# Batch 0's phi by halves, its score copies on two engines, its second FFN1 in P's banks, and a last store in halves

## The chip, the core and the metric

The kernel runs on one core of a Trainium2 chip. The metric is the device time of one execution in microseconds (us); of several executions the median counts. Of the core's engines four matter: TensorE (PE, matmuls and transpositions), VectorE (DVE) and ScalarE (ACT), which convert, copy and do the pointwise work, and SyncE (SP), whose queue issues nearly all transfers. Each engine works through its own queue in order and waits there for what the others have to deliver.

## The reference

For 8 batches of 576 rows and 8 heads, 32 weights phi per row are turned by a softmax over all of the sequence into 32 mean keys and values per head; the rows attend to these means, and the result, 4608 rows of 512, goes through an FFN of width 2048 with SiLU.

```
a = phi - np.max(phi, axis=2, keepdims=True)
a = np.exp(a)
a = a / (np.sum(a, axis=2, keepdims=True) + 1e-09)
k_m = np.einsum('bhsm,bhsd->bhmd', a, k)
v_m = np.einsum('bhsm,bhsd->bhmd', a, v)
scores = scale * np.matmul(q, k_m.transpose(0, 1, 3, 2))
...
attn = attn / (np.sum(attn, axis=-1, keepdims=True) + 1e-09)
x = np.matmul(attn, v_m)          # then rows of 512 = heads x 64
h = x @ w_in
g = h * (1.0 / (1.0 + np.exp(-h)))
return g @ w_out
```

## The kernel before, in words

**The FFN sets the frame.** The kernel goes through the 8 batches, and in each through 16 slices of 128 columns of the FFN's width, called fc. For a slice, *FFN1* (ffn1, L593) makes the 128 hidden units for all 576 rows: two halves of 288 columns, six matmuls each, since every operand is split into a high and a low part and three of the products are needed. ScalarE applies the SiLU (silu, L613 for 512 rows; L615 for the 64 rows left over, into *gleft*), VectorE splits the result into a high and a low part (split, L605 and L607), and *FFN2* (ffn2, L627) adds 4 tiles x 3 matmuls to the accumulators *acc*. FFN2 of a slice runs behind FFN1 of the next one (prev, finish). The rows left over of two batches are gathered and done at the end of every second batch (left_step); a finished accumulator is copied out by ScalarE and stored over SP's queue (store, L633 and L636).

**P instead of x @ w_in.** x is attention times mean values, and so the kernel multiplies the mean values with w_in first: *P* (p_mm, L563, 16 matmuls into the two banks *bg*) has 32 rows per head. ScalarE writes its high part (L577), VectorE its low part (L579), both into *pparts*. FFN1 then multiplies pparts with the attention *aparts*, also in two parts. In batch 0, P is made in pieces of 256 columns, each of which needs one tile of w_in.

**The weights** come as 64-bit words and are converted on the chip during batch 0. w_in has eight tiles i0 to i7, w_out o0 to o7, of 256 of the 2048 hidden units each. The steps of a tile are called by letters (w_conv): p (L166) and c (L168) on ScalarE, s (L170) and a (L172) on VectorE, and for w_out also h (L174, *wo_hi*) on ScalarE and l (L176, *wo_lo*) on VectorE. I0 and O0 are converted in halves 0 and 1. The words land in three buffers *raw*; load_next issues a tile's load on SP when its place in the program is reached, and a load into a buffer waits until the conversion that reads it is done.

**Batch 0's attention** stands at the head of the program. *phi_max*, *phi_allmax* make a maximum over the sequence for each of the two halves p of phi (two transpositions and a broadcast on TensorE, L252 and L258), *phi_sub* (L291) subtracts it, *phi_exp* (L299, L302) takes the exponential, *e_mm* makes the mean keys and values (72 matmuls, L311 and L319) and divides them (L335, *kvn*). *f_tr* and *f_vt* transpose these (*kvT*). *f_scores(u)* (L448) makes the scores of half u of the rows, *f_copy(u)* (L461 for 2x256 columns into *sT*, L462 for the small rest into *sleft*) copies them out of PSUM, *f_turn(u)* (L473, L475) transposes them. Then come maximum, shift, exponential, sum and division (*f_max* L496, *f_sub* L501, *f_exp* L507, *f_sum* L511 to L513, *f_norm* L517), the way back (*f_back* L524, L532) and the two parts of the attention (*f_high* L542, *f_low* L545). The first FFN1 needs both. Between these, *keep_warm* (L79) gives TensorE matmuls whose result is not used.

**What sets the order.** The head of the program is a list of calls written out by hand (from L719). in_order ties the instructions of VectorE and ScalarE there to the order of the list, and those of TensorE and SP as well. Behind it, from slice 2 of batch 0, a table of slots (ev, events) says behind which half slice a piece of the next batch's attention, of P or a conversion (conv_next) stands; there a scheduler puts the instructions of VectorE and ScalarE in order, while TensorE and SP keep the program's order until the end of batch 0.

## Time and profile before

| | |
|---|---|
| median of 3 runs | 713.25 us (713.0 to 713.45) |
| the profiled execution | 711.86 us, its span 710.1 us |
| TensorE busy | 696.2 us, 98% of the span |
| VectorE busy | 366.3 us, 52% |
| ScalarE busy | 258.5 us, 36% |
| bytes moved | 60.14 MB, 85 GB/s on the mean |

The span runs from the first to the last instruction in the trace, and all times in it count from its start; the 1.76 us between span and execution lie around it. TensorE's busy share is an average over the whole span; the views below go by stretch. In a timeline a row stands for one instruction or a few of a kind in a row; "[1.70 <-ACT sleft L462]" says that the engine was idle for 1.70 us ahead of it, until ScalarE's L462 was done. Starts of neighbouring rows overlap a little, as instructions are pipelined.

### The profile page before, as it was taken

How to read it: one execution, taken by the hardware profiler on the slowest of the kernel's cores; microseconds unless marked ns; L12 is line 12 of the kernel's file. 1: busy time of each engine (PE TensorE's matmuls, PEld its weight loads, DVE VectorE, ACT ScalarE, POOL GpSimd, SP SyncE). 2: the span in 40 equal slices, each digit the busy share in tenths (PEclk: the TensorE clock that was granted, in tenths of full speed). 3: DMA queues.
4: the chain of work that ended last, by engine and by line, in shares of the span. 5: the costliest groups of instructions: out<-in, count | busy, mean ns of one | idle time of the engine just before them, and what ended most of it. 6: DMA issues, size and time to landing. Idle time of an engine off the chain costs nothing.

```text
span 710.1 us, 11571 instructions
## 1 busy us (share of the span) xinstructions
PE 696.2 (98%) x4833; PEld 556.1 (78%) x4833; DVE 366.3 (52%) x658; ACT 258.5 (36%) x454; POOL 0.7 (0%) x6
## 2 busy tenths in 40 slices
PE   7899999999999999999999999999999999999997
PEld 3577678788888788777887778887888878888885
DVE  3899886355353563538246373535635356233322
ACT  2789854233323332424224241423322323222211
POOL 0000000000000000000000000000000000000000
PEclk9999999999999999999999999999999999999999
DMA  9977615321113210232011420132101000010002
GB/s 341 387 243 235 245 38 224 135 67 35 45 31 135 67 34 1 83 146 68 1 60 20 153 76 3 61 135 67 34 15 60 2 1 1 0 61 1 1 1 74
DMA packets 25444, 60.14 MB, mean 85 GB/s; under 512 B 2096, under 2 KB 10416, under 8 KB 25392
## 3 DMA queue, kind: packets, MB, share of 16 engines
q1 hardware_dynamic: 24672, 57.02, 23.0%
q10 hardware_dynamic: 720, 2.38, 0.9%
q8 instruction: 38, 0.62, 0.4%
q14 instruction: 14, 0.11, 0.1%
HBM read 49.95 MB, written 9.44 MB: 84 GB/s over the span
## 4 chain that ended last, share of the span: by engine, by line
PE 83%; DVE 3%; ACT 2%; DMA 1%; issue 0%; ACTq 0%
PE acc L627 44%; PE h L593 25%; PE accleft L627 6%; PE bg L563 4%; PE bg L311 2%; PE bg L357 1%; DMA raw<-in_w_out 1%; DVE gparts L607 1%; ACT L613 1%; DVE phi L291 1%; ACT phi L299 0%; ACT pparts L577 0%; PE bg L319 0%; DVE qz L275 0%; ACT g L613 0%
## 5 line engine op out<-in xcount | busy, mean ns | idle before, releaser
L627 PE MATMUL acc<-wo_hi,gparts 128*128 128x512 f32 x1024 | 352.5, 397 | 0.3 <-DVE gparts L607 0.3
L627 PEld LDWEIGHTS acc<-wo_hi,gparts 128*128 128x128 f32 x1024 | 191.9, 188 | 66.9 <-issue 29.8
L593 PEld LDWEIGHTS h<-aparts,pparts 128*128 128x128 f32 x1536 | 215.2, 188 | 17.8 <-ACT gleft L615 4.7
L593 PE MATMUL h<-aparts,pparts 128*128 128x288 f32 x1536 | 225.9, 296 | 1.6 <-ACT gleft L615 0.8
L627 PE MATMUL acc<-wo_lo,gparts 128*128 128x512 f32 x512 | 201.2, 393 | 0.4 <-DVE wo_lo L176 0.4
L613 ACT ACTIVATE g<-h 128x512 f32<-128x512 f32 x128 | 76.4, 597 | 303.4 <-issue 175.4
L605 DVE CAST gparts<-g 128x512 fp32r<-128x512 f32 x128 | 54.5, 426 | 222.0 <-ACT g L613 221.2
L627 PEld LDWEIGHTS acc<-wo_lo,gparts 128*128 128x128 f32 x512 | 96.1, 188 | 15.2 <-DVE wo_lo L176 0.7
L607 DVE TENSOR_TENSOR gparts<-g,gparts 128x512 fp32r<-128x512 f32 x128 | 88.2, 689 | 10.5 <-DVE gparts L605 0.5
L579 DVE TENSOR_TENSOR pparts<-bg,pparts 128x1024 fp32r<-128x1024 f32 (+1 forms) x36 | 39.6, 1099 | 36.2 <-ACT pparts L577 36.2
L577 ACT ACTIVATE pparts<-bg 128x1024 fp32r<-128x1024 f32 (+1 forms) x36 | 33.4, 927 | 27.8 <-PE bg L563 27.8
L627 PE MATMUL accleft<-wo_hi,gparts 128*128 128x512 f32 x128 | 40.6, 389 | 0.0
L563 PE MATMUL bg<-win,kvT 64*32 64x512 f32 (+1 forms) x576 | 35.8, 554 | 0.9 <-DVE kvn L335 0.9
L615 ACT ACTIVATE gleft<-h 128x64 f32<-128x64 f32 x128 | 28.0, 218 | 0.0
L627 PEld LDWEIGHTS accleft<-wo_hi,gparts 128*128 128x128 f32 x128 | 24.0, 188 | 4.9
L633 ACT ACTIVATE o<-acc 128x512 f32<-128x512 f32 x32 | 19.2, 599 | 21.9 <-PE acc L627 10.7
L627 PE MATMUL accleft<-wo_lo,gparts 128*128 128x512 f32 x64 | 24.9, 389 | 0.0
L613 ACT ACT_TABLE_LOAD x14 | 18.0, 1283 | 8.0 <-PE h L593 7.9
L563 PEld LDWEIGHTS bg<-win,kvT 64*32 64x32 f32 x576 | 6.5, 104 | 14.1 <-issue 11.7
L605 DVE CAST gparts<-gleft 128x512 fp32r<-128x512 f32 x16 | 6.8, 427 | 20.3 <-PE accleft L627 11.9
L168 ACT ACTIVATE raw<-raw 128x1024 int32<-128x1024 uint32 (+1 forms) x16 | 16.7, 1041 | 0.0
L395 DVE TENSOR_REDUCE ssm<-sc 128x36 f32<-128x1152 f32 x7 | 9.5, 1354 | 8.8 <-ACT sc L391 8.8
(126 smaller groups left out, 365.6 us busy)
## 6 DMA issues: line engine op xcount, KB each, us to landing
kv<-in_kv SPq DMA_DIRECT2D x28, 516.0 KB, 5.7
q<-in_q SPq DMA_DIRECT2D x16, 576.0 KB, 3.8
out<-o SPq DMA_DIRECT2D x32, 256.0 KB, 2.1
raw<-in_w_in SPq DMA_DIRECT2D x14, 512.0 KB, 6.4
raw<-in_w_out SPq DMA_DIRECT2D x6, 1024.0 KB, 7.3
phi<-in_phi SPq DMA_DIRECT2D x7, 576.0 KB, 3.7
kv<-in_kv ACTq DMA_DIRECT2D x4, 516.0 KB, 6.0
kr<-in_kv SPq DMA_DIRECT2D x7, 258.0 KB, 7.2
```

The lines of the kernel that those rows point to most:

```text
L168: nc.scalar.activation(r, low, AF.Copy, scale=2.0**-29)
L311: nc.tensor.matmul(pt[p][M * r : M * (r + 1), :KVW], e[:, p, c, M * r : M * (r + 1)], kvt[c][:, p, r], start=c == 0, stop=False, skip_grou ...
L563: nc.tensor.matmul(bg[M * r : M * (r + 1), p, :w].rearrange("p (k f) -> p k f", f=P), kvT[D * p : D * (p + 1), 1, r], win[D * p : D * (p + ...
L577: nc.scalar.activation(hi[:, :, c], bg[:, :, :w], AF.Copy)
L579: nc.vector.tensor_tensor(lo[:, :, c], bg[:, :, :w], hi[:, :, c], op=ALU.subtract)
L593: nc.tensor.matmul(h[:, hf, :HALF], wt[:, p, fs], a[:, p, sl], start=n == 0, stop=n == 5)
L605: nc.vector.tensor_copy(ghi, g32)
L607: nc.vector.tensor_tensor(glo, g32, ghi, op=ALU.subtract)
L613: nc.scalar.activation(g32.rearrange("p (h f) -> p h f", h=2), h[:, :, :w], AF.Silu)
L615: nc.scalar.activation(gleft[:, fc, o : o + LEFT].rearrange("p (h f) -> p h f", h=2), h[:, :, w:HALF], AF.Silu)
L627: nc.tensor.matmul(acc[key], gt[:, cs], wt[:, fc], start=fc == 0 and n == 0, stop=fc == NFC - 1 and n == 2)
L633: nc.scalar.activation(o, acc.pop(key), AF.Copy)
```

## The change

In batch 0, phi's second half is no longer held back: each half is shifted and exponentiated right behind its own maximum (phi_sub works half by half, in all batches), and e_mm multiplies half 0 ahead of half 1. One of the two divisions goes to ScalarE. A half's scores are copied by ScalarE (256 columns and the rest) and VectorE (256 columns). The order of the list is another one: the warm-up matmuls are spread differently, both turns come ahead of f_vt, I0's second half is converted behind f_norm(0), O0's second half partly behind the first FFN1, I1 behind the second silu. The first FFN1 does the products with the attention's low part last (low_last), and the second FFN1 writes into the banks bg of P in place of h. On SP's queue the first load_next of three, w_in's tile 3, stands ahead of phi(1), the other two ahead of kv(1) and q(1, 0). The last store of the kernel is copied by ScalarE and VectorE, half each, and its two transfers go over the queues of SP and of ScalarE.

```
     def phi_sub(b, ps_=(0, 1)):
...
+        for p in ps_:
+            am = at[b]["am", p]
+            nc.vector.tensor_tensor(
+                e[:, p], e[:, p], am.unsqueeze(1).broadcast_to([P, FULLC, P]), op=ALU.subtract
+            )
+            nc.vector.tensor_tensor(er[rows(p)], er[rows(p)], am[rows(p)], op=ALU.subtract)
...
         turns = [(c, p) for c in range(FULLC) for p in range(2)]
+        if b == 0:
+            turns.sort(key=lambda t: t[1])
...
-            if b and p == 0:
+            if p == (b == 0):
                 nc.scalar.activation(kvn[:, :, p], src, AF.Copy, scale=rs[p])
...
-        nc.scalar.copy(t, first["st", u][:, :, : 2 * P])
+        nc.scalar.copy(t[:, 0], first["st", u][:, 0, : 2 * P])
+        nc.vector.tensor_copy(t[:, 1], first["st", u][:, 1, : 2 * P])
...
+    def ffn1(b, fc, h=None, low_last=False):
...
+        if h is None:
+            h = live["h"] = ps.tile([P, 2, 512], F32, tag="h", name="h", bufs=1)
+        kinds = ((hi, ahi), (hi, alo), (lo, ahi))
+        todo = [(hf, k) for hf in range(2) for k in range(3)]
+        if low_last:
+            todo = [(hf, k) for k in (0, 2, 1) for hf in range(2)]
...
+    def store(key, rows, last=False):
...
+        w = DMODEL // 2 if last else DMODEL
+        nc.scalar.activation(o[:, :w], a[:, :w], AF.Copy)
+        if last:
+            nc.vector.tensor_copy(o[:, w:], a[:, w:])
...
+            (nc.scalar if last and k else nc.sync).dma_start(out[r : r + n], o[at_ : at_ + n])
...
         for p in range(2):
             phi_max(0, (p,))
             phi_allmax(0, (p,))
-            keep_warm(idle, (5, 6)[p])
-        for p in range(2):
             phi_sub(0, (p,))
             phi_exp(0, (p,))
+            keep_warm(idle, (5, 2)[p])
         e_mm(0)
...
         f_copy(0)
-        w_conv(I0, 1, "pc")
+        keep_warm(idle, 2)
         f_turn(0)
         f_scores(1)
         f_copy(1)
-        f_vt()
-        f_turn(1)
+        spare = ps.tile([P, 512], F32, tag="acc", name="spare", bufs=NI)
+        keep_warm(spare, 2)
         f_max(0)
         f_sub(0)
-        w_conv(I0, 1, "sa")
+        f_turn(1)
+        f_vt()
         f_exp(0)
...
         f_sum(0)
+        f_norm(0)
+        w_conv(I0, 1, "pc")
+        f_back(0)
+        f_sum(1)
+        w_conv(I0, 1, "sa")
+        f_high(0)
+        w_conv(O0, 0, "pc")
+        keep_warm(spare, 7)
+        bg = p_mm(0, 0, CW, False)
         p_split(0, 0, CW, bg, (0,))
...
+        w_conv(O0, 0, "ha")
+        w_conv(O0, 1, "p")
+        h = ffn1(0, 0, low_last=True)
+        w_conv(O0, 0, "l")
+        gs = split(silu(0, 0, h))
+        w_conv(O0, 1, "c")
+        g32 = silu(0, 1, ffn1(0, 1, bgtile()))
+        w_conv(I1, None, "pcsa")
+        main_step(0, 0, gs, (0, 1))
+        g1 = split(g32, steps=(0,))
+        p_mm(0, CW, CW)
         w_conv(O0, 1, "sh")
...
+    load_next()
     load_phi(1)
+    load_next()
+    load_next()
     load_kv(1)
     load_q(1, 0)
-    for _ in range(3):
-        load_next()
```

What the new order does to the queues shows at three places.

**ScalarE from the first wo_hi to P's second piece.** The two rows of L613 (L626 now) are the silus of the first two slices; "L166 ... win<-raw 128x1024" and the L168 on raw 128x1024 are I1's two steps, and L577 (L582 now) writes P's high part. Before:

```order
L174 ACTIVATE wo_hi<-cva 128x512
L166 ACTIVATE win<-raw 128x1024
L613 ACTIVATE g_359<-h 128x512
L615 ACTIVATE gleft<-h 128x64
L168 ACTIVATE raw<-raw 128x1024
L174 ACTIVATE wo_hi<-cva 128x512
L613 ACTIVATE g_382<-h 128x512
L615 ACTIVATE gleft<-h 128x64
L577 ACTIVATE pparts<-bg 128x2x256
```

After:

```order
L174 ACTIVATE wo_hi<-cva 128x512
L166 ACTIVATE cva<-raw 128x512
L626 ACTIVATE g_355<-h 128x512
L628 ACTIVATE gleft<-h 128x64
L168 ACTIVATE raw<-raw 128x512
L626 ACTIVATE g_374<-bg 128x512
L628 ACTIVATE gleft<-bg 128x64
L166 ACTIVATE win<-raw 128x1024
L168 ACTIVATE raw<-raw 128x1024
L582 ACTIVATE pparts<-bg 128x2x256
L174 ACTIVATE wo_hi<-cva 128x512
```

I1's first step stood ahead of the first silu and its second step between the two silus; both now stand behind the second silu. O0's second wo_hi moved from ahead of the second silu to behind P's high part.

**VectorE from behind the first shift of the scores to the second division.** "fmx" and "fsc ... fmx" are f_max and f_sub, "fsm" and "fsc<-fsc,fsm" are f_sum and f_norm; "L170 win" and "L172 win" are the steps of I0's second half. Before:

```order
L170 TENSOR_SCALAR win<-win 128x512
L172 ISA win<-raw,win 128x1024
L496 TENSOR_REDUCE fmx<-firstu 128x20
L501 TENSOR_TENSOR fsc<-firstu,fmx 128x640
L511 TENSOR_REDUCE fsm<-fsc 128x16
L512 TENSOR_SCALAR fsm<-fsm 128x16
L513 RECIPROCAL fsm<-fsm 128x16
L517 TENSOR_TENSOR fsc<-fsc,fsm 128x512
L511 TENSOR_REDUCE fsm<-fsc 128x20
L512 TENSOR_SCALAR fsm<-fsm 128x20
L513 RECIPROCAL fsm<-fsm 128x20
L517 TENSOR_TENSOR fsc<-fsc,fsm 128x640
```

After:

```order
L501 TENSOR_REDUCE fmx<-firstu 128x20
L506 TENSOR_TENSOR fsc<-firstu,fmx 128x640
L516 TENSOR_REDUCE fsm<-fsc 128x16
L517 TENSOR_SCALAR fsm<-fsm 128x16
L518 RECIPROCAL fsm<-fsm 128x16
L522 TENSOR_TENSOR fsc<-fsc,fsm 128x512
L516 TENSOR_REDUCE fsm<-fsc 128x20
L517 TENSOR_SCALAR fsm<-fsm 128x20
L518 RECIPROCAL fsm<-fsm 128x20
L170 TENSOR_SCALAR win<-win 128x512
L172 ISA win<-raw,win 128x1024
L522 TENSOR_TENSOR fsc<-fsc,fsm 128x640
```

I0's two steps moved from ahead of f_max(1) to between f_sum(1) and f_norm(1).

**The score copies, with the semaphores that each waits for.** "Activation" is ScalarE's semaphore, "DVE" VectorE's, "PE" TensorE's, and "DMAHW" a transfer's; "sT" takes the scores' 2x256 columns and "sleft" the rest. ScalarE before:

```order
L461 COPY sT_233<-bg 128x512 [waits DMAHW3_49,PE_49]
L462 COPY sleft<-bg 128x2x32
L166 ACTIVATE win<-raw 128x512 [waits DMAHW3_49]
L168 ACTIVATE raw<-raw 128x512
L461 COPY sT_252<-firsts 128x512 [waits DMAHW4_49,PE_49]
L462 COPY sleft<-firsts 128x2x32
L441 COPY kvT_215<-firstt 128x128 [waits DVE_49]
```

ScalarE after:

```order
L465 COPY sT_228<-bg 128x256 [waits DMAHW3_49,PE_49]
L467 COPY sleft<-bg 128x2x32 [waits DVE_49]
L465 COPY sT_248<-firsts 128x256 [waits DMAHW4_49,PE_49]
L467 COPY sleft<-firsts 128x2x32 [waits DVE_49]
L445 COPY kvT_210<-firstt 128x128
```

VectorE after:

```order
L170 TENSOR_SCALAR win<-win 128x512 [waits Activation_49]
L172 ISA win<-raw,win 128x1024 [waits DMAHW6_49,DVE_49,Activation_49]
L466 COPY sT_228<-bg 128x256 [waits DMAHW3_49,Activation_49]
L466 COPY sT_248<-firsts 128x256 [waits DMAHW4_49,Activation_49]
L501 TENSOR_REDUCE fmx<-firstu 128x16
```

ScalarE's one copy per half has become a copy on ScalarE and one on VectorE; VectorE's waits for ScalarE, and ScalarE's copy of the rest waits for VectorE.

## Rows read from the trace of the kernel before

**Rows 1.** Page, parts 1 and 2: busy time by engine; clock by slice.

```profile
PE 696.2 (98%) x4833; PEld 556.1 (78%) x4833; DVE 366.3 (52%) x658; ACT 258.5 (36%) x454; POOL 0.7 (0%) x6
...
PEclk9999999999999999999999999999999999999999
```

**Rows 2.** Windows: length; busy time (instructions) PE, PEld, DVE, ACT, POOL; clock; DMA.

```profile
42.00:75.00 33.00, 31.83 (x270) 25.37 (x262) 29.95 (x49) 28.84 (x38) 0.00 (x0) 1.00 0.66 214
...
75.00:110.00 35.00, 34.55 (x259) 26.30 (x260) 30.34 (x43) 21.96 (x34) 0.00 (x0) 1.00 0.43 153
```

**Rows 3.** Timeline, TensorE, 0 to 20: start, length, instruction, idle before.

```profile
1.35 4.42 PE L79 MATMUL idle<-ident 128*128 128x512 bf16 x11 [1.35 <-POOL ident masks.py:199]
...
6.27 0.49 PE L258 MATMUL firstm<-ident,cm 128*128 128x128 f32 x2 [0.38 <-DVE cm L253]
...
11.04 1.75 PE L311 MATMUL first<-kv,phi 128*32 128x129 f32 x56 [0.36 <-ACT phi L302]
...
17.31 0.71 PE L448 MATMUL firsts<-q,kvT 64*32 64x288 f32 x16
...
19.73 0.66 PE L473 MATMUL firstu<-ident,sT 128*128 128x128 f32 x4 [1.70 <-ACT sleft L462]
```

**Rows 4.** Timeline, VectorE, 6 to 26.

```profile
6.13 0.42 DVE L240 TENSOR_TENSOR mt<-phi 128x256 f32<-128x256 f32 x1
...
13.72 0.61 DVE L335 TENSOR_SCALAR kvn<-first,rs 128x128 f32<-128x128 f32 x2
...
19.29 0.69 DVE L172 CUSTOM_DVE_ANT_0 win<-raw,win 128x1024 uint16<-128x1024 uint16 x1
...
25.32 0.83 DVE L517 TENSOR_TENSOR fsc<-fsc,fsm 128x640 f32<-128x640 f32 x1
```

**Rows 5.** Timeline, ScalarE, 17 to 24.

```profile
17.87 0.66 ACT L166 ACTIVATE win<-raw 128x512 f32<-128x512 f32 x1 [1.08 <-DMA raw<-in_w_in]
...
18.98 0.59 ACT L461 COPY sT<-firsts 128x512 f32<-128x512 f32 x1
...
19.55 0.29 ACT L441 COPY kvT<-firstt 128x128 f32<-128x128 f32 x1
...
23.00 1.28 ACT L755 ACT_TABLE_LOAD   x1
```

**Rows 6.** Timeline, TensorE, 27 to 44.

```profile
27.77 0.53 PE L593 MATMUL h<-aparts,pparts 128*128 128x288 f32 x2
...
30.91 1.85 PE L593 MATMUL h<-aparts,pparts 128*128 128x288 f32 x12 [0.80 <-ACT gleft L615]
...
32.60 0.39 PE L627 MATMUL acc<-wo_hi,gparts 128*128 128x512 f32 x1
...
34.08 0.66 PE L563 MATMUL bg<-win,kvT 64*32 64x256 f32 x16
...
42.01 1.85 PE L593 MATMUL h<-aparts,pparts 128*128 128x288 f32 x12
```

**Rows 7.** Timeline, ScalarE, 35 to 42.

```profile
35.85 1.14 ACT L166 ACTIVATE win<-win 128x1024 f32<-128x1024 f32 x1
...
40.00 0.62 ACT L613 ACTIVATE g<-h 128x512 f32<-128x512 f32 x1
...
41.43 0.25 ACT L615 ACTIVATE gleft<-h 128x64 f32<-128x64 f32 x1
```

**Rows 8.** Timeline, VectorE, 32 to 34.

```profile
32.66 1.23 DVE L172 CUSTOM_DVE_ANT_0 win<-raw,win 128x2048 uint16<-128x2048 uint16 x1
```

**Rows 9.** Timeline, ScalarE and then TensorE, 72 to 76.

```profile
72.18 1.14 ACT L166 ACTIVATE cva<-raw 128x1024 f32<-128x1024 f32 x1 [0.93 <-DMA raw<-in_w_out]
...
75.05 0.67 PE L563 MATMUL bg<-win,kvT 64*32 64x256 f32 x16 [0.85 <-DVE kvn L335]
```

**Rows 10.** Timeline, all engines and queues, from 705.

```profile
705.49 0.60 ACT L633 ACTIVATE o<-accleft 128x512 f32<-128x512 f32 x1 [9.61 <-PE accleft L627]
...
706.11 1.11 SPq L636 DMA_DIRECT2D out<-o  x2
```

More of the change, by code (lines that the diff above doesn't have):

```diff
@@ L586, in ffn1 @@
         ahi, alo = at[b]["ahi"], at[b]["alo"]
-        h = live["h"] = ps.tile([P, 2, 512], F32, tag="h", name="h", bufs=1)
-        for hf in range(2):
-            sl = slice(hf * HALF, (hf + 1) * HALF)
-            n = 0
-            for wt, a in ((hi, ahi), (hi, alo), (lo, ahi)):
-                for p in range(2):
-                    nc.tensor.matmul(h[:, hf, :HALF], wt[:, p, fs], a[:, p, sl], start=n == 0, stop=n == 5)
-                    n += 1
+        if h is None:
[4 more added lines that the diff above has]
+            todo = [(hf, k) for k in (0, 2, 1) for hf in range(2)]
+        n = [0, 0]
+        for hf, k in todo:
+            wt, a = kinds[k]
+            for p in range(2):
+                nc.tensor.matmul(
+                    h[:, hf, :HALF], wt[:, p, fs], a[:, p, hf * HALF : (hf + 1) * HALF],
+                    start=n[hf] == 0, stop=n[hf] == 5, skip_group_check=low_last,
+                )
+                n[hf] += 1
         return h
@@ L648, in left_step @@
         if n == NLS - 1:
[L649 removed]
+            store((b, "left"), [((b - 1) * S + MAIN, LEFT), (b * S + MAIN, LEFT)], b == B - 1)
     events = {}
@@ L724, in attn_ffn_kernel @@
             phi_allmax(0, (p,))
-            keep_warm(idle, (5, 6)[p])
-        for p in range(2):
             phi_sub(0, (p,))
             phi_exp(0, (p,))
+            keep_warm(idle, (5, 2)[p])
         e_mm(0)
         w_conv(I0, 0, "pc")
-        keep_warm(idle, 4)
+        keep_warm(idle, 3)
         f_tr()
```

47 lines of the change are left out of this document (10 added, 37 removed).

## The prediction

> **What bounds the kernel now.** I began with the page's busy shares: TensorE is busy for 98% of the span, at the full clock in every slice [rows 1]. The windows show where batch 0 and the start of batch 1 lose time: TensorE is idle for 1.17 us between 42 and 75 and for 0.45 between 75 and 110 [rows 2]; before 28 us much of what it runs are warm-up matmuls. So the time is a fixed stream of matmuls plus the moment at which that stream flows freely. An edit to batch 0 counts only by how much it shifts the FFN1 at 42.01 [rows 6], or a later one; a gain that a later wait swallows is worth nothing. I therefore read TensorE, VectorE and ScalarE in order of time through batch 0 and followed every step that the new order moves.
>
> **Phi by halves, and the means of k and v.** Half 0's broadcast is written at 6.27 + 0.49 = 6.76 [rows 3], so its shift can run there, and no longer only behind both halves' maxima. It now stands ahead of half 1's maxima (from 6.13 until now [rows 4]), which delays half 1's shift by between 0 and 0.9, the shift's own length with its remainder; I take 0.4, half of it, because TensorE was still busy with warm-up matmuls when half 1's maxima were done. Against that, half 0's 16 matmuls are done by then: 16 instead of 28 stand behind half 1's exponential, and 12 x 0.06 us (1.75 for 56 records, two a matmul [rows 3]) is 0.7. Net −0.3. The division, two in a row on VectorE (0.61 for both [rows 4]), now has one on each engine: −0.3. So the scores start 0.6 sooner.
>
> **The score copies.** ScalarE copied 512 columns in 0.59; 128 columns took 0.29 [rows 5], so 256 take about 0.39, and VectorE needs 0.42 for 256 columns [rows 4]. The changed program makes VectorE's copy wait for ScalarE's, and the small copy of the left part for VectorE's. So each pair costs 0.81 in a row, +0.2 each time; the copy by two engines doesn't do what it says.
>
> The Trainium skill (PSUM — Partial Sum Buffer, Specifications) says that ScalarE and VectorE can read PSUM in parallel as long as they keep to different banks. By it each pair would take 0.42 and f_max(1) would come 0.4 sooner; no row here shows the two side by side, and the program's own waits forbid it.
>
> What does help is that the conversion of I0's second half is gone from there: it waited 1.08 for its landing and held the second copy until 18.98 [rows 5], though the scores were written at 17.31 + 0.71 = 18.02 [rows 3]. Now the copies start at 18.02 − 0.6 + 0.2 + 0.1 = 17.7 and end at 18.55; before it was 19.57, so −1.0. On VectorE f_max(0) and f_sub(0) come only behind that second copy, for about 0.69 each (128x512 at that engine's pace for 640 columns, 0.83 [rows 4]), so f_max(1) starts near 19.85. Before, the turn that it reads ended at 19.73 + 0.66 = 20.4 [rows 3], its small part and the step to VectorE 0.1 later: −0.7 is left.
>
> **The moved conversion takes that back.** I0's second half now stands behind the table load, which ended at 23.00 + 1.28 [rows 5] and now ends 0.7 sooner, at 23.6. ScalarE's two conversions (0.66 each, the second starting 0.1 before the first ends) end at 24.85, VectorE's step (0.69 [rows 4]) at 25.6, and f_norm(1) waits behind it: 25.5 instead of 25.32. So the first FFN1, at 27.77 [rows 6], starts near 28.0: **the whole gain of 0.7 is gone, +0.2.**
>
> **Two FFN1s in a row.** The first no longer pauses for the low part of the attention, and the second has banks of its own, so it doesn't wait for the silu as it did (0.80 idle at 30.91 [rows 6]). With 1.69 a piece (30.91 to the first FFN2 at 32.60) the second ends at 28.0 + 3.4 = 31.4, against 32.6. −1.2 here; nothing has been given back yet.
>
> **The new wait.** P's next matmuls (34.08 [rows 6]) need w_in's tile I1. Before, its first conversion lay ahead of the first silu and its second right behind it, and VectorE's last step of it ran at 32.66 for 1.23 [rows 8]: ready at 33.9, when TensorE got there. Now all of I1 stands behind the second silu on ScalarE. From 31.5: silu 0.6 (0.62 [rows 7]; its left part ends beside the next step), two conversions at 1.04 (four of them fill 35.85 to 40.00 [rows 7]) and 0.1 for the last one's end, then VectorE 1.23 and 0.1 to TensorE: 31.5 + 0.6 + 2.1 + 0.1 + 1.23 + 0.1 = 35.6. P's matmuls are 1.5 later than before. TensorE has six FFN2 matmuls (1.48, 32.60 to 34.08) to fill 31.4 to 35.6 and stands idle for 2.7. Queued behind the wait are the other six FFN2s, and on the two other engines all that reads P.
>
> **What follows on ScalarE.** P is written at 35.6 + 0.66 + 0.1 = 36.35; its high part takes ScalarE 0.6 (128x512, as the silu [rows 7]), until 36.95, its low part VectorE 0.7 (a 128x512 of two inputs, as above), until 37.65, then the shift of O0's second half 0.4, and only then ScalarE's wo_hi 0.6, until 38.65. The four conversions of i2 and o1 follow (4.15): 42.7. From the silu that stands behind them to the end of the left part there were 1.68 us (40.00 to 41.43 + 0.25 [rows 7]), now until 44.35. The FFN1 that waits for that left part's banks starts at 44.4 instead of 42.01: **+2.4**. Before, the left part ended 0.3 ahead of that FFN1, so none of this is hidden. VectorE's wo_lo for O0, behind the same wait, also comes late, but ends sooner than this chain.
>
> **Loads.** On SP's queue i3, phi(1), o2 and i4 now stand ahead of kv(1) and q(1,0). i3 waits for the conversion of I0 (25.6), o2 for I1's (35.5), i4 for O0's; kv(1) and q(1,0) follow near 40 and are read only by batch 1's steps. i3 lands sooner but is converted behind o1 all the same; later tiles wait for buffers that come free with the late conversions. What this can give back is bounded: nothing at one end, at the other the 1.17 + 0.45 that TensorE idles between 42 and 110 [rows 2]. An example of it is 75.05, where it waited 0.85 because ScalarE had stood 0.93 for a landing at 72.18 [rows 9]. Modelled ends hide part of what is lost there, so for the range I allow twice the sum, 3.2. I take 0.5, near the lower end: the conversions keep their distance to the stream.
>
> **The tail.** The last copy takes 0.60 at 705.49, and two store issues on one queue 1.11 from 706.11 [rows 10]. The copy in halves is again one behind the other (0.39 + 0.42, +0.2), and both stores wait for the second half, but they issue together and save about 0.55: −0.35, between 0 and −0.55. Shifting later batches' phi in two pieces costs VectorE 0.1 a batch, beside a TensorE that is busy.
>
> **The sum.** 2.4 − 0.5 − 0.35 = +1.55. The profiled execution took 711.86 with a span of 710.1; it becomes 713.4. It is 1.4 below the median of the runs, 713.25, so the forecast for that is 714.8.
>
> **The rivals.**
> *The weights' stage gives more back.* ScalarE there stops waiting for landings, since i3 and o2 come without kv(1) and q(1,0) ahead of them. With all of the visible 1.6: 2.4 − 1.6 − 0.35, 713.7. For it speaks rows 9; against it that buffers come free late.
> *Faster.* The same place from a further point on: if every o tile has landed before ScalarE asks for it, nothing between 42 and 110 holds TensorE, and up to 3.2 comes back: 2.4 − 3.2 − 0.35 = −1.15, 712.1. It decides at the o tile that held ScalarE at 72.18: this landing must come a microsecond sooner against ScalarE's own order. Against it: its load is issued when an earlier tile's conversion ends, and that is later.
> *Worse.* These landings slip by as much as the stream, and ScalarE, now with the late conversions close behind each other, holds a silu: one more wait like 75.05's, +0.85, and no gain: 2.4 + 0.85 − 0.35, 716.1.
> *The clock.* Full clock is granted in every slice [rows 1], and TensorE's longest pause was 1.70, ahead of the second turn [rows 3]. The new pause is 2.7. If TensorE falls there from 2.4 to 1.2 GHz, and for as long as the first eleven warm-ups took, 4.42 (0.40 each [rows 3], though the record's clock is full there), half of that is lost: +2.2, 717.0.
>
> The Trainium skill (TensorE: Matmul & The Clock Gate, What's actually happening) says that the chip halves this clock after an idle stretch and gives it back after sustained work. By it the 2.7 may or may not be enough; nothing before shows a pause of that length.
>
> **How the numbers follow.** My forecast 0.44 (714.8, its own range 713.9 to 715.8), more given back 0.24 (713.7), faster 0.13 (712.1), worse 0.12 (716.1), the clock 0.07 (717.0). A measurement of this kernel tells about 0.2% from no change, that is 1.43 us: 711.8 and 714.7 are the borders. Faster holds most of its own rival, 0.10; slower the two last and a bit over half of the forecast, 0.47; 0.43 is left for no change. The range of 712.3 to 716.5 leaves out half of the fastest case and the clock's, with a little of the worse one.
>
> **What would show it.** VectorE's score copies start where ScalarE's end. f_norm(1) stands right behind an L172 near 25.5. TensorE idles for over 2 us until about 35.5, released by VectorE's L172 on win, and over 1 us ahead of the FFN1 near 44.4, released by gleft. From there the FFN1s of batch 0 are 1 to 3 us late, constant from about 95 on. The last two stores issue at the same time. I am wrong if the wait near 35.5 is under 1 us, or if the FFN1 after 95 stands where it stood.

## The result, and the profile after

The changed kernel took 715.4 us (median of 8 runs, 714.9 to 717.03), the kernel before 713.21 in the same runs (712.18 to 713.99). The ratio is 1.0034, with a 95% interval of 1.0023 to 1.0045: slower, by a little more than a measurement can tell from no change. The forecast was 714.8. The profiled execution of the changed kernel took 715.28, with a span of 713.5.

The page of the changed kernel, parts 1 and 2, answers to [rows 1]:

```profile
PE 696.6 (98%) x4829; PEld 557.6 (78%) x4829; DVE 368.2 (52%) x667; ACT 259.2 (36%) x455; POOL 0.7 (0%) x6
...
PEclk9989999999999999999999999999999999999999
```

TensorE is as busy as before, 696.6 us against 696.2. So the 3.4 us between the two spans are idle time and slow matmuls, and one digit of the clock line, the third, is below 9. The windows of the changed kernel (columns as in [rows 2], with one stretch more) show where:

```profile
33.00:42.00 9.00, 6.47 (x35) 5.12 (x36) 6.59 (x10) 5.30 (x7) 0.00 (x0) 0.62 0.39 127
42.00:75.00 33.00, 33.00 (x285) 26.75 (x284) 30.04 (x49) 29.35 (x39) 0.00 (x0) 1.00 0.80 280
75.00:110.00 35.00, 33.05 (x248) 24.68 (x247) 31.13 (x45) 24.14 (x35) 0.00 (x0) 1.00 0.42 149
```

From 33 to 42 us TensorE is idle for 2.53 us, and its mean granted clock is 0.62: for part of that stretch it ran at 1.2 GHz. From 42 to 75, where 1.17 us were idle before, none is; from 75 to 110 it is 1.95 in place of 0.45. TensorE's timeline tells the same (start, length, instruction, idle before and its releaser):

```profile
27.89 1.87 PE L603 MATMUL h<-aparts,pparts 128*128 128x288 f32 x12 [0.75 <-ACT aparts L547]
29.60 1.76 PE L603 MATMUL bg<-aparts,pparts 128*128 128x288 f32 x12
...
35.53 1.11 PE L568 MATMUL bg<-win,kvT 64*32 64x256 f32 x16 [2.70 <-DVE win L172]
...
39.29 2.79 PE L603 MATMUL h<-aparts,pparts 128*128 128x288 f32 x12
...
45.37 1.85 PE L603 MATMUL h<-aparts,pparts 128*128 128x288 f32 x12
...
82.14 0.44 PE L349 MATMUL h<-ident,kvn 128*128 128x128 f32 x2 [1.65 <-ACT gleft L628]
```

The first two FFN1s stand one behind the other, at 27.89 and 29.60, and end 1.4 us sooner than in [rows 6], where FFN2 began at 32.60 (now 31.19). Then P's second piece at 35.53 waits 2.70 us for VectorE's L172 on win, I1's last step; in [rows 6] it stood at 34.08, without a wait. It takes 1.11 in place of 0.66, and the FFN1 behind it, slice 2's, 2.79 in place of 1.93: these matmuls ran at the lower clock. The FFN1 of slice 3 starts at 45.37 in place of 42.01, with no wait ahead of it. And at 82.14 there is a wait of 1.65 us that the kernel before did not have.

ScalarE in the same kernel, around the pause and ahead of slice 3:

```profile
31.99 1.12 ACT L166 ACTIVATE win<-raw 128x1024 f32<-128x1024 f32 x1
32.99 1.13 ACT L168 ACTIVATE raw<-raw 128x1024 int32<-128x1024 uint32 x1
...
43.15 0.60 ACT L626 ACTIVATE g<-h 128x512 f32<-128x512 f32 x1
...
44.57 0.23 ACT L628 ACTIVATE gleft<-h 128x64 f32<-128x64 f32 x1
```

and VectorE's step that releases TensorE:

```profile
34.16 1.23 DVE L172 CUSTOM_DVE_ANT_0 win<-raw,win 128x2048 uint16<-128x2048 uint16 x1 [0.32 <-ACT raw L168]
```

I1's two steps on ScalarE run from 31.99, right behind the second silu, to 34.12; VectorE's last step begins at 34.16 and ends at 35.39. [rows 8] had it at 32.66. Slice 2's left part is done at 44.80, 0.57 ahead of slice 3's FFN1.

How far the stream of matmuls lies behind, slice by slice, is read from the starts of the FFN1s (timelines of TensorE; the kernel "before, tail" is an experiment below, whose batch 0 is that of the kernel before):

| FFN1 of batch 0's slice | before | before, tail | after | after against before |
|---|---|---|---|---|
| 0 | 27.77 | 28.43 | 27.89 | +0.12 |
| 2 | 36.17 | 36.84 | 39.29 | +3.12 |
| 3 | 42.01 | 42.66 | 45.37 | +3.36 |
| 9 | 75.64 | 76.72 | 77.24 | +1.60 |
| 10 | 81.98 | 83.08 | 84.86 | +2.88 |
| last of the kernel | 687.32 | 688.39 | 690.84 | +3.52 |

The profiled execution of the kernel before was an early one: VectorE's maximum of phi's second half began at 6.13 without waiting for its landing [rows 4], while in the two other profiles with this head (two experiments below) it began at 7.79 and 7.98, after waits of 1.01 and 1.68 for it. "Before, tail" is 0.66 later at slice 0 and 1.10 at slice 10. That is most of the 1.35 us by which this profile lay under the median, and why the profiles differ by 3.4 us and the medians by 2.2.

### The profile page after: what moved, and what is told of

The parts are those of the page before. It is cut to its first block, busy times and chain, and to the rows that moved or that the text cites. A ratio compares the mean times of both kernels' runs of the same rounds, so it can differ in the third digit from the quotient of the medians.

```text
span 713.5 us, 11577 instructions
## 1 busy us (share of the span) xinstructions
PE 696.6 (98%) x4829; PEld 557.6 (78%) x4829; DVE 368.2 (52%) x667; ACT 259.2 (36%) x455; POOL 0.7 (0%) x6
## 4 chain that ended last, share of the span: by engine, by line
PE 77%; DVE 8%; ACT 5%; issue 1%; DMA 1%; ACTq 0%; DVEq 0%
PE acc L640 42%; PE h L603 24%; PE accleft L640 5%; PE bg L568 3%; PE bg L315 2%; DVE gparts L620 1%; ACT L626 1%; PE bg L361 1%; DVE phi L294 1%; ACT phi L301 1%; ACT g L626 1%; DMA raw<-in_w_out 1%; ACT pparts L582 1%; DVE gparts L618 1%; DVE qz L276 1%
## 5 line engine op out<-in xcount | busy, mean ns | idle before, releaser
L626 ACT ACTIVATE g<-h 128x512 f32<-128x512 f32 x127 | 75.9, 598 | 305.5 <-issue 175.4
L582 ACT ACTIVATE pparts<-bg 128x1024 fp32r<-128x1024 f32 (+1 forms) x36 | 33.4, 927 | 30.9 <-PE bg L568 30.9
L168 ACT ACTIVATE raw<-raw 128x1024 int32<-128x1024 uint32 (+1 forms) x16 | 16.7, 1046 | 0.0
```

The lines of the kernel that those rows point to most:

```text
L168: nc.scalar.activation(r, low, AF.Copy, scale=2.0**-29)
L582: nc.scalar.activation(hi[:, :, c], bg[:, :, :w], AF.Copy)
L626: nc.scalar.activation(g32.rearrange("p (h f) -> p h f", h=2), h[:, :, :w], AF.Silu)
```

## The experiments

In all of them the ratio is to the kernel before, run on the same chip.

### I1 sooner again

```
         w_conv(O0, 1, "p")
+        w_conv(I1, None, "p")
         h = ffn1(0, 0, low_last=True)
...
         w_conv(O0, 1, "c")
+        w_conv(I1, None, "csa")
         g32 = silu(0, 1, ffn1(0, 1, bgtile()))
-        w_conv(I1, None, "pcsa")
```

> The changed kernel with one part undone: I1's first ScalarE step stands ahead of the first silu and its second between the two silus, as before the change. Theory (I1 behind the second silu sets the 2.70 us pause at 35.53, and the half-rate stretch from 34.77 to 41.60 follows from that pause): the pause shrinks to about 1 us, P's second piece starts near 33.7, the clock stays at 2.4 GHz, the FFN1 of slice 3 starts near 42.9 in place of 45.37, and the time falls by 2 to 2.9 us, to 712.5 to 713.4. Rival (the loads' new order sets the time further on, at the 1.65 us wait at 82.14): the gain at slice 3 is swallowed there, and the time falls by less than 0.8 us, to 714.6 or more.

It took 713.69 us; the ratio is 1.0013 (1.0004 to 1.0022), against the changed kernel's 1.0034 a gain of 1.5 us. That lies between the two forecasts. TensorE's timeline:

```profile
33.84 0.67 PE L568 MATMUL bg<-win,kvT 64*32 64x256 f32 x16 [0.83 <-DVE win L172]
...
42.66 1.85 PE L603 MATMUL h<-aparts,pparts 128*128 128x288 f32 x12 [0.97 <-ACT gleft L628]
...
79.65 0.45 PE L349 MATMUL h<-ident,kvn 128*128 128x128 f32 x2 [2.19 <-ACT gleft L628]
```

and a window behind the last of these rows:

```profile
75.00:84.00 9.00, 6.81 (x42) 4.39 (x41) 7.21 (x10) 6.49 (x10) 0.00 (x0) 0.81 0.88 320
```

The pause is 0.83 in place of 2.70, P's piece starts at 33.84, and slice 3 at 42.66, 2.7 sooner. Up to there the theory holds. But at 79.65 the wait for gleft has grown from 1.65 to 2.19, and behind it the clock fell (0.81 on the mean of 75 to 84). The rival was right that part of the gain is swallowed there, though not most of it: slice 10 is still 1.4 nearer to the first FFN1 than in the changed kernel (55.59 against 56.97). The fall of the clock is not in every execution: of the eleven, eight had a granted clock of 0.999 or 1.0 on the mean of the whole execution, and three, the profiled one among them, 0.996 or 0.997.

### Warm-up matmuls in the pause

```
+        gap = ps.tile([P, 512], F32, tag="acc", name="gap", bufs=NI)
+        keep_warm(gap, 11)
         p_mm(0, CW, CW)
```

> The changed kernel with 11 more warm-up matmuls (a result that nobody reads, into a free accumulator bank) ahead of P's second piece, so that TensorE is busy in the pause before 35.53 and nothing else moves. It separates the pause from the clock. Theory (the clock fell because of the pause, but ScalarE's chain bounds slice 3 anyway): P's second piece still starts near 35.5, the clock stays at 2.4 GHz, the FFN1 of slice 3 starts at 44.4 to 44.9 in place of 45.37 and waits there for gleft, and the time falls by 0.4 to 1.0 us. Rival (the clock is most of the loss): 6.07 us at half rate come back, 3 us, and the time is that of the kernel before. Second rival (the clock fell for another reason than the pause): the half-rate stretch stays and the time with it.

715.34 us, ratio 1.0039 (1.0027 to 1.0051): no gain. TensorE's timeline, and the window of the pause:

```profile
33.40 2.55 PE L79 MATMUL gap<-ident 128*128 128x512 bf16 x11
36.31 0.67 PE L568 MATMUL bg<-win,kvT 64*32 64x256 f32 x16 [0.36 <-DVE win L172]
...
45.13 1.05 PE L603 MATMUL h<-aparts,pparts 128*128 128x288 f32 x6 [0.98 <-ACT gleft L628]
```

```profile
33.00:42.00 9.00, 8.25 (x54) 5.27 (x53) 6.27 (x10) 5.75 (x7) 0.00 (x0) 1.00 0.37 122
```

The clock stays full, and P's piece takes 0.67 again. This execution's first FFN1 stands at 28.62, so distances from there compare: slice 3 comes 16.51 behind it, against 17.48 in the changed kernel (45.37 − 27.89). The fall of the clock thus cost 0.97 at slice 3, as expected, and now TensorE waits there, 0.98 for gleft. But at slice 10 only 0.3 is left (56.65 against 56.97, timelines), and in the time nothing that the two intervals could tell. So the pause was the clock's cause in this place, and most of the clock's price was hidden by waits further on: the first rival is out, and so is the second; the theory holds at slice 3 and fails at the end.

### The loads in their old order

```
-    load_next()
     load_phi(1)
-    load_next()
-    load_next()
     load_kv(1)
     load_q(1, 0)
+    for _ in range(3):
+        load_next()
```

> The changed kernel with the loads behind the list in the order of before: phi(1), kv(1), q(1,0), then three tiles of weights. Theory formed from the changed kernel's trace (the new order brings i3 and o2 sooner, which gives 1.76 us back between 45 and 77, but brings kv(1) later, which costs 1.29 at 82.14): FFN1s up to slice 9 are 0.4 to 1.0 later than in the changed kernel, the wait at 82.14 goes, and the time falls by 0.8 to 1.4 us, to 714.0 to 714.6. Rival (the prediction's: the order gives back about 0.5 and nothing is lost to it): the time rises by 0.5, to 715.9.

713.79 us, ratio 1.0014 (1.0004 to 1.0025): by the ratios 1.4 less than the changed kernel, as the theory formed after the result has it, and against the prediction. TensorE's timeline:

```profile
36.24 1.11 PE L568 MATMUL bg<-win,kvT 64*32 64x256 f32 x16 [2.71 <-DVE win L172]
...
81.21 0.44 PE L349 MATMUL h<-ident,kvn 128*128 128x128 f32 x2 [0.32 <-ACT gleft L628]
```

The pause is still 2.71, and P's piece again takes 1.11; but the wait that stood at 82.14 is 0.32. Slice 9 comes no later: 49.05 behind the first FFN1 (77.64 − 28.59), against 49.35 in the changed kernel. But the low clock lasted less long here (0.81 on the mean of 33 to 42, in place of 0.62), so the way from the FFN1 of slice 3 to that of slice 9 compares better: 32.14, against 31.87 in the changed kernel. The first experiment and the next but one ("Both undone") differ by the order of the loads alone, and their clock was full up to slice 9: 31.56 with the new order, 32.25 with the old. So the sooner i3 and o2 give back 0.3 to 0.7 there and not the 1.76 of the theory; the rest has another source (below). The other half holds. In the changed kernel the loads of kv(1) are issued at 41.4, between the weights' tiles, and not at 21.7. The transfer of w_out that was issued next to them (out<-in, engine, count, KB each, us to landing) took in the changed kernel

```profile
raw<-in_w_out SPq DMA_DIRECT2D x1, 1024.0 KB, 7.8
```

and with the old order

```profile
raw<-in_w_out SPq DMA_DIRECT2D x1, 1024.0 KB, 4.9
```

at nearly the same time of issue, 50.36 and 50.16. From 48 to 50 the DMA engines were busy all the time in the changed kernel (share 1.00) and idle with the old order (0.00). ScalarE in the changed kernel:

```profile
58.24 1.15 ACT L166 ACTIVATE cva<-raw 128x1024 f32<-128x1024 f32 x1 [0.78 <-DMA raw<-in_w_out]
...
80.38 1.12 ACT L168 ACTIVATE raw<-raw 128x1024 int32<-128x1024 uint32 x1
81.40 0.58 ACT L626 ACTIVATE g<-h 128x512 f32<-128x512 f32 x1
```

It waits for the late tile and begins that conversion at 58.24; with the old order that step ran at 55.16. Every tile behind it is then converted later, until the silu of slice 9 stands behind the two steps of another conversion: it starts 4.16 behind the start of its FFN1 (77.24), with the old order 2.80 (80.44 and 77.64), and TensorE stands at 82.14.

### I1 later in the kernel before

```
-        w_conv(I1, None, "p")
         gs = split(silu(0, 0, ffn1(0, 0)))
-        w_conv(I1, None, "csa")
         w_conv(O0, 1, "sh")
         g32 = silu(0, 1, ffn1(0, 1))
+        w_conv(I1, None, "pcsa")
```

> The kernel before with one part of the change alone: all of I1's conversion behind the second silu. Theory: P's second piece (34.08 before) waits for I1, TensorE stands for about 2.5 us near 36, the FFN1 of slice 3 starts 2.4 us later or more, near 44.4, and the time rises by 2 to 3.5 us, to 715.2 to 716.7, with a half-rate stretch behind the pause if the pause is as long as in the changed kernel. Rival (the pause is covered by slack that lies further on, in the loads): the time rises by under 0.7 us.

715.08 us, ratio 1.0033 (1.002 to 1.0046): this part alone makes the kernel before as slow as the whole change does. TensorE's timeline and the window:

```profile
37.73 0.67 PE L563 MATMUL bg<-win,kvT 64*32 64x256 f32 x16 [2.71 <-DVE win L172]
```

```profile
35.00:42.00 7.00, 4.28 (x37) 3.25 (x37) 5.09 (x8) 4.92 (x6) 0.00 (x0) 1.00 0.98 349
```

A pause of 2.71, released by the same L172. The clock stayed full in this execution, though the pause is as long as in the changed kernel. Slice 3 starts 16.51 behind the first FFN1 (45.13 − 28.62), 2.27 more than the 14.24 of the kernel before (42.01 − 27.77): the 2.4 of the forecast, from this part alone.

### Both undone

The edits of the first and the third experiment together.

> The changed kernel with two parts undone at once: I1's conversion as before the change (a1) and the order of the loads as before (a3). Theory (two separate losses, the pause at 35.53 and the wait at 82.14, and each hides behind the other when only one is undone): the FFN1 of slice 3 starts about 0.7 later than in the kernel before, the one of slice 10 about 1.2 sooner, no pause over 1.2 us is left behind 30, the clock stays at 2.4 GHz, and the time is 1.0 to 1.6 us below that of the kernel before, 711.4 to 712.2. Rival (the new order of batch 0 itself is late, whatever is undone): the time stays above the kernel before, 713.3 or more, as in a1 and a3 alone.

711.68 us, ratio 0.9988 (0.9979 to 0.9997): faster than the kernel before. TensorE's timeline:

```profile
34.31 0.67 PE L568 MATMUL bg<-win,kvT 64*32 64x256 f32 x16 [0.85 <-DVE win L172]
...
43.12 1.85 PE L603 MATMUL h<-aparts,pparts 128*128 128x288 f32 x12 [0.99 <-ACT gleft L628]
...
79.14 0.44 PE L349 MATMUL h<-ident,kvn 128*128 128x128 f32 x2 [0.52 <-ACT gleft L628]
```

Behind 30 no pause is over 1 us, and the clock stays full. From its first FFN1 (28.46) slice 3 comes 14.66 later, 0.42 more than in the kernel before, and slice 10 comes 53.09 later in place of 54.21. Against the changed kernel's ratio of 1.0034, one part undone took off 0.0021, the other 0.0020, and both together 0.0046. So two losses made the result, I1 behind the second silu and the loads, and they add up rather than hide each other; without them the rest of the change is a small gain.

### The score copies side by side

To the kernel above, with the last accumulator copied by ScalarE alone and its two stores on two queues:

```
+            t = [ps.tile([P, 512], F32, tag="acc", name=f"firsts{p}", bufs=NI) for p in range(2)]
...
+        nc.scalar.copy(t[:, 0], st[0][:, : 2 * P])
+        nc.vector.tensor_copy(t[:, 1], st[1][:, : 2 * P])
+        nc.scalar.copy(lv[:, 0, u], st[0][:, 2 * P : HALF])
+        nc.vector.tensor_copy(lv[:, 1, u], st[1][:, 2 * P : HALF])
```

> The kernel of the run above with two more edits. The scores of the second half are written into two tiles of one PSUM bank each in place of one tile of two, so that the program lets ScalarE's and VectorE's copies run side by side; and the last accumulator is copied by ScalarE alone, its two stores still on two queues. Theory (the copies were serialised only because both read one tile): VectorE's copy of the second half starts within 0.1 us of ScalarE's in place of 0.40 behind it, the first FFN1 starts 0.3 to 0.45 sooner, the end of the last matmul to the end of the span shrinks by 0.2 to 0.3, and the time is 0.5 to 0.75 below that run, 710.8 to 711.6. Rival (the two engines read PSUM one after the other anyway): the copies overlap in the program but take longer each, to about 0.8 for the pair, and the first FFN1 starts at the same time.

711.74 us, ratio 0.9983 (0.9973 to 0.9992). The two copies of the second half, ScalarE's and VectorE's:

```profile
18.21 0.37 ACT L471 COPY sT<-firsts 128x256 f32<-128x256 f32 x1 [1.12 <-PE firsts L456]
```

```profile
18.25 0.42 DVE L472 COPY sT<-firsts 128x256 f32<-128x256 f32 x1 [0.94 <-DMA raw<-in_w_out]
```

They run side by side and take 0.37 and 0.42, as long as one behind the other in the changed kernel (below). So the wait came from the one tile that both read, not from the chip. The Trainium skill (PSUM — Partial Sum Buffer, Specifications) says that ScalarE and VectorE can read PSUM in parallel as long as they keep to different banks; this trace agrees, with these two durations. The first FFN1 came 0.25 sooner than in the run above (28.21), with phi's second half at the same time (8.05 and 8.08), a little less than expected, and that was lost again: at slice 10 TensorE waits, which it did not above.

```profile
82.82 1.86 PE L610 MATMUL h<-aparts,pparts 128*128 128x288 f32 x12 [1.02 <-ACT kvT L351]
```

### I0's second half in its old place

```
         f_copy(0)
+        w_conv(I0, 1, "pc")
...
         f_sub(0)
+        w_conv(I0, 1, "sa")
...
-        w_conv(I0, 1, "pc")
         f_back(0)
         f_sum(1)
-        w_conv(I0, 1, "sa")
```

> The changed kernel with I0's second half converted where it was before the change: its ScalarE steps behind the first score copy, its VectorE steps behind the first shift. Theory of the prediction (the moved conversion takes back the gain of 0.7 ahead of f_norm(1)): without it f_norm(1) comes 0.5 to 0.9 sooner, the first FFN1 starts near 27.4 and the time falls by up to 0.5. Rival (the old place is worse in the new order, since the words of that half land near 17.6 only, and ScalarE's second score copy then waits behind them): the second copy ends 1 to 2 us later, the first FFN1 starts near 29.5 to 30, and the time rises by 1.5 to 2.5, to 717 or more.

717.56 us, ratio 1.0064 (1.0047 to 1.008): the rival was right. ScalarE's first step of that half, and TensorE around it:

```profile
18.46 0.66 ACT L166 ACTIVATE win<-raw 128x512 f32<-128x512 f32 x1 [1.90 <-DMA raw<-in_w_in]
```

```profile
20.68 0.65 PE L478 MATMUL firstu<-ident,sT 128*128 128x128 f32 x4 [2.58 <-ACT sleft L467]
...
21.28 4.66 PE L79 MATMUL spare<-ident 128*128 128x512 bf16 x13
```

The words land only at 18.46, ScalarE's copy of the second scores stands behind that step, and TensorE waits 2.58 for it. The clock fell there (0.66 on the mean of 21 to 26): thirteen warm-up matmuls take 4.66 us. In the changed kernel they took 2.97:

```profile
19.35 2.97 PE L79 MATMUL spare<-ident 128*128 128x512 bf16 x13
```

The first FFN1 starts at 30.48.

### The halved last store alone

The part of the change in store, in the kernel before.

> The kernel before with the halved last store alone. Theory: batch 0 stays as it is; behind the last matmul ScalarE's copy of 256 columns (0.39) and VectorE's (0.42) stand one behind the other, the two stores issue together 0.9 behind the start of the first copy, and from the start of the copy to the end of the span it is 0.1 to 0.35 shorter than in the kernel before (4.61 from 705.49 to 710.10). Rival: the two queues' stores land no sooner than one queue's, and that stretch is as long or longer by the 0.25 that the copies add.

One execution of 712.8 us, span 711.0. Its end:

```profile
706.57 0.39 ACT L635 ACTIVATE o<-accleft 128x256 f32<-128x256 f32 x1 [9.61 <-PE accleft L627]
706.99 0.42 DVE L637 COPY o<-accleft 128x256 f32<-128x256 f32 x1 [4.84 <-ACT o L635]
707.44 0.47 SPq L640 DMA_DIRECT2D out<-o  x1
```

VectorE's copy stands behind ScalarE's, as the program's waits say. From the first copy's start to the end of the span it takes 4.43 in place of 4.61 (705.49 to 710.10). The copies cost 0.25 more (0.87 to the issue in place of 0.62) and the stores end 0.43 sooner behind their issue (3.56 in place of 3.99).

### One FFN1 at a time

Two kernels: the one with I1 and the loads as before, and the changed kernel, each with the second FFN1 in h, behind the first silu, as in the kernel before:

```
-        h = ffn1(0, 0, low_last=True)
+        h = ffn1(0, 0)
...
-        g32 = silu(0, 1, ffn1(0, 1, bgtile()))
+        g32 = silu(0, 1, ffn1(0, 1))
```

> The kernel with I1 and the loads as before the change (c1), and with the second FFN1 also as before: it writes into h, behind the first silu, and the first FFN1 does its products in the old order. It measures what two FFN1s in a row are worth. Theory (ScalarE's chain sets slice 3, so that most of the 1.2 us is hidden): the second FFN1 starts 1.5 later, P's second piece about 0.5 later, the FFN1 of slice 3 about 0.5 later, and the time is 0.3 to 0.6 above c1 (0.9988 of the kernel before), near 0.9995. Rival (all of it is on TensorE's path): slice 3 and the end come 1.2 later than in c1, and the time is 0.5 above the kernel before.

> The changed kernel with the second FFN1 alone as before: it writes into h, behind the first silu, and the first FFN1 does its products in the old order. Theory (with I1 behind the second silu everything waits for that silu, so there the 1.2 us are on the path): the silu, I1's conversion, P's second piece and the FFN1 of slice 3 all come 1.2 to 1.6 later than in the changed kernel (11.40 from the first FFN1 to that of slice 2, 17.48 to that of slice 3). Rival (ScalarE's chain hides it here too): under 0.6 later at slice 3.

The first took 712.2 us, ratio 0.9991 (0.9982 to 1.0). The second, in one execution, took 716.25. TensorE in the first:

```profile
31.90 1.86 PE L603 MATMUL h<-aparts,pparts 128*128 128x288 f32 x12 [0.80 <-ACT gleft L628]
...
43.93 1.85 PE L603 MATMUL h<-aparts,pparts 128*128 128x288 f32 x12 [0.98 <-ACT gleft L628]
```

and in the second:

```profile
46.30 1.85 PE L603 MATMUL h<-aparts,pparts 128*128 128x288 f32 x12 [0.98 <-ACT gleft L628]
```

In the first, slice 3 starts 15.17 behind the first FFN1 (28.76), 0.51 later than with the two FFN1s in a row (14.66): of the 1.4 that they win at the second FFN1 (3.14 behind the first, in place of 1.71 in the changed kernel), 0.9 is hidden behind ScalarE. In the times the two kernels can't be told apart (0.9991 and 0.9988). In the second kernel P's second piece comes 9.11 behind the first FFN1 (28.35), 1.47 later than in the changed kernel (7.64), as the theory has it. Slice 3 is at 17.95, only 0.47 later than the 17.48 that the forecast compared with, for the changed kernel's clock fell in its pause and here it stayed full through one of 2.71; against the kernel with warm-ups in the pause, where the clock was full too (16.51), it is 1.44. The changed kernel needs the two in a row, since there all that follows waits for the second silu. Both theories hold at these places, the second only with the clock's part taken out.

### Phi's shift in one piece

Two last kernels: phi's shift in one piece again in batches 2 to 7, in the kernel with the side-by-side copies, and in the one with I1 and the loads as before, there with the last copy on ScalarE alone.

```
+            at[b]["am"] = am.rearrange("p (g f) -> p g f", g=2)
...
     def phi_sub(b, ps_=(0, 1)):
         e, er = at[b]["e"], at[b]["er"]
+        if "am" in at[b]:
+            nc.vector.tensor_tensor(
+                e, e, at[b]["am"].unsqueeze(2).broadcast_to([P, 2, FULLC, P]), op=ALU.subtract
+            )
...
+            return
         for p in ps_:
```

and in store, in both:

```
-        nc.scalar.activation(o[:, :w], a[:, :w], AF.Copy)
-        if last:
-            nc.vector.tensor_copy(o[:, w:], a[:, w:])
+        nc.scalar.activation(o, a, AF.Copy)
```

> The kernel d6 (I1 and loads as before the change, the second half's scores in two tiles, the last copy on ScalarE alone with two stores) with the shift of phi in one piece again in batches 2 to 7, as before the change; batches 0 and 1 keep it by halves. Theory (the two pieces let other work of VectorE come between them, and in batch 2 a silu then comes 0.44 late at TensorE's FFN1 near 217): that wait goes, the stretch from slice 20 to the last FFN1 is 0.3 to 0.6 shorter than in d6, and the time falls by as much, to 0.9975 to 0.998 of the kernel before. Rival (that wait comes from batch 1 and stays): no difference to d6 within 0.1%.

> The kernel c1 (I1 and loads as before the change) with the shift of phi in one piece in batches 2 to 7 and the last accumulator copied by ScalarE alone, its two stores on two queues; the scores' copies are as in the changed kernel. Beside h1 it tells what the side-by-side copies are worth at the end. Theory (what they gain ahead of the first FFN1, 0.25, is lost to waits for loads near 75 and 82): the same time as h1 within 0.1%, and the end behind the last copy's start is 4.2 in place of 4.49. Rival: 0.25 to 0.5 slower than h1.

They took 711.15 us, ratio 0.9977 (0.9968 to 0.9986), and 711.31, ratio 0.9979 (0.997 to 0.9988). In the first, the stretch from slice 4 of batch 1 (slice 20 of the kernel) to the last FFN1 is 554.17, 0.60 shorter than with two pieces (554.77 in the kernel with the side-by-side copies), as expected. The two are equal: what the side-by-side copies win ahead of the first FFN1 is gone at the end. The tail, from the last copy's start to the end of the span, is 4.27 and 4.22. Both kernels beat the kernel before and the changed one.

## Why the prediction was right, and where it was not

**The head.** The scores start at 14.61 in place of 15.27, 0.66 sooner (forecast 0.6), although phi landed later in this execution. The copies of the second half stand one behind the other. ScalarE's two, and VectorE's with the conversion and the division further on, in the changed kernel:

```profile
17.62 0.37 ACT L465 COPY sT<-firsts 128x256 f32<-128x256 f32 x1 [1.11 <-PE firsts L452]
18.48 0.21 ACT L467 COPY sleft<-firsts 128x64 f32<-128x64 f32 x1 [0.49 <-DVE sT L466]
```

```profile
18.02 0.42 DVE L466 COPY sT<-firsts 128x256 f32<-128x256 f32 x1 [1.76 <-ACT sT L465]
...
24.83 0.69 DVE L172 CUSTOM_DVE_ANT_0 win<-raw,win 128x1024 uint16<-128x1024 uint16 x1
25.44 0.82 DVE L522 TENSOR_TENSOR fsc<-fsc,fsm 128x640 f32<-128x640 f32 x1
```

VectorE's copy starts at 18.02, where ScalarE's ends, and the small one behind it ends at 18.69 (forecast 18.55). f_norm(1) stands at 25.44 (25.5), right behind an L172, and the first FFN1 at 27.89 (28.0). The step's reading was too narrow, though: it said that the moved conversion "takes that back", as if the old place were free. In the new order the old place is worse: there the first FFN1 stands at 30.48, 2.6 later, with phi's second half at the same time (7.51 and 7.46), because the words land late. And the +0.2 came out (+0.12) against a profile whose phi landed early. From the maximum of phi's second half to the first FFN1 it takes 20.43 in the changed kernel (27.89 − 7.46), and in both profiles of the old head that waited for phi 20.64 (28.43 − 7.79 and 28.62 − 7.98): for the same landing the new head is 0.2 shorter.

**The two FFN1s, the new wait, and ScalarE's chain.** The second FFN1 ends at 31.19 (31.4); the wait is 2.70 (2.7) and ends at 35.53 (35.6). With the clock full, slice 3 stands 16.51 behind the first FFN1; the forecast was 44.4 − 28.0 = 16.4. That part of the sum was right step by step, and moving I1 in the kernel before showed it alone.

**The clock.** It was a rival with 0.07, at 2.2 us. It fell, in the profile and by the granted clock of 0.995 to 0.997 in all eight executions, and so the forecast wait of over 1 us ahead of slice 3 is not there: slow matmuls fill it. Its price was mis-sized: 0.97 at slice 3, 0.3 at slice 10, and in the time nothing that the intervals tell, since TensorE had to wait for ScalarE there anyway. The Trainium skill (TensorE: Matmul & The Clock Gate, What's actually happening) says that the chip halves this clock after an idle stretch; the trace agrees, with pauses of 2.70, 2.71, 2.72 and 2.58 us that did it. It did not follow in the profiles of the two other kernels with a pause of 2.71, and one of 2.19 was enough once.

**What is given back.** This step failed, though its number came out: 0.5 forecast, 0.48 measured from slice 3 to slice 10 (3.36 to 2.88). It was two things: 1.76 given back up to slice 9, as "the weights' stage gives more back" had it, and 1.29 lost at 82.14, where it expected nothing new. The 1.76 are only in part the loads' doing, as that rival put it. From the FFN1 of slice 3 to that of slice 9 it takes (timelines of TensorE):

| kernel | order of the loads | slice 3 to 9 | slice 9 to 10 |
|---|---|---|---|
| before | old | 33.63 | 6.34 |
| before, tail | old | 34.06 | 6.36 |
| I1 later in the kernel before | old | 33.63 | 6.21 |
| changed, loads in their old order | old | 32.14 | 5.98 |
| both undone | old | 32.25 | 6.18 |
| changed | new | 31.87 | 7.62 |
| changed, I1 sooner again | new | 31.56 | 9.38 |

A stream that is only later, by I1, wins nothing up to slice 9. The rest of the change wins over 1 us there with the old order of the loads, where the kernel before idled for 1.17 [rows 2], and the new order adds 0.3 to 0.7; which other part of the change wins the 1 us isn't shown. The new order then loses 1.6 and 3.2 at slice 10. Its sentence on kv(1) and q(1, 0), that they are read only by batch 1's steps, looked at who reads them; what counted was what they stood beside on their way.

**The tail.** −0.35 forecast, −0.12 measured (4.49 from the first copy's start to the end, in place of 4.61). The end of the changed kernel:

```profile
709.01 0.39 ACT L648 ACTIVATE o<-accleft 128x256 f32<-128x256 f32 x1 [9.61 <-PE accleft L640]
709.43 0.42 DVE L650 COPY o<-accleft 128x256 f32<-128x256 f32 x1 [4.84 <-ACT o L648]
709.88 0.47 SPq L653 DMA_DIRECT2D out<-o  x1
709.89 0.55 ACTq L653 DMA_DIRECT2D out<-o  x1
```

The copies cost 0.25 (forecast 0.2); the mis-sized term is the stores, which save 0.37 (3.62 behind the issue in place of 3.99), not 0.55.

**The later batches.** "Beside a TensorE that is busy" was wrong at one place, slice 3 of batch 2:

```profile
219.44 1.86 PE L603 MATMUL h<-aparts,pparts 128*128 128x288 f32 x12 [0.44 <-ACT gleft L628]
```

The exponential and a silu come later there, and 0.44 is lost; the experiment with one piece has no such wait. But the two pieces don't make it alone. Three kernels that have them together with the old order of the loads ("The loads in their old order", "Both undone" and the first of "One FFN1 at a time") do not wait there either: from slice 20 to the last FFN1 they take 554.42, with one piece it is 554.14 to 554.17, and with the wait 554.77 in the changed kernel. So two pieces cost 0.25, and the wait 0.35 more. All five profiles with the new order of the loads have it, and of those with the old order and two pieces only the one with side-by-side copies. In these six VectorE's split between the two pieces starts 0.26 to 0.28 late; what holds it isn't shown.

**The anchor.** 1.4 us were added for the distance from profile to median. The change by profile was 3.4, not 1.55; by median 2.2. The profile of before was early in its first loads, so the change came out 1.85 above the sum, and from the changed kernel's profile to its median 0.1 was left in place of 1.4: the two errors partly cancelled. By the kernel "before, tail" the step to slice 3 is 2.71, and to the last FFN1 2.45. That the forecast came within 0.6 of the median is therefore in part luck. The working has a slip of 0.1 besides: 38.65 and 4.15 make 42.8 and not 42.7.

**What stays open.** In the profiles of the four fastest kernels, which are nearly equal up to slice 8, slice 10 comes 53.09, 53.77, 54.13 and 54.61 behind the first FFN1. So where exactly the fast ones win near there, in the landings or in ScalarE's order, isn't settled by one profile each. Nor is why the same pause lowered the clock in one profile and not in another. It differs between executions of one kernel too: with I1 later in the kernel before, the granted clock of the five was 0.999, 0.997, 0.999, 0.997 and 0.996. But the kernel before itself, whose profile has no pause over 1.70 in batch 0, went from 0.995 to 1.0, so the mean over an execution doesn't say at which pause the clock fell.

## What to carry to other kernels

A conversion that is moved behind a later step must still end ahead of the matmul that reads it: write down its reader and that reader's time before moving it. A gain ahead of a chain that ends later is worth what is left at the chain's end, here 0.5 of 1.4. When loads are put in another order, look at what flies beside them, not only at who reads them.

## What was not expected of the hardware

The same transfer of 1 MB took 4.9 us to land in one kernel and 7.8 in another, issued at the same point, with the DMA engines idle just before in the one (share 0.00) and busy in the other (1.00). A pause of TensorE of 2.7 us was followed by the lower clock in the profiles of three kernels and not in those of two. ScalarE's and VectorE's copies out of two PSUM banks at once took 0.37 and 0.42, as long as alone.
